# Weight loads moved behind the last row sums, and a lower pace for the mixing between the heads, in a fused attention and mixing kernel

## The chip, the cores and the metric

The kernel runs on one core of one Trainium2 chip. The metric is the device time of one execution in microseconds (us); lower is better. Engines are named as in the profile: PE is TensorE (matmuls; PEld are its weight loads), DVE is VectorE, ACT is ScalarE, POOL is GpSimd, and SP is the engine whose queue issues most of the DMAs.

## What is computed

Three steps follow each other. First comes causal attention with a decay bias, for 4 batches of 8 heads, 576 positions and 64 channels a head. Then a gated mixing with a convolution of five taps, and a second mixing with a product over positions, both on 4 x 576 x 512 numbers:

```python
cum = np.cumsum(np.maximum(s, 0.0), axis=-1)
scores = np.where(causal, -1e9, scale * (q @ k.T) + np.minimum(-(cum[..., :, None] - cum[..., None, :]), 0.0))
attn = softmax(scores)            # exp, divided by the row sums + 1e-9
x = attn @ v                      # heads side by side: [4, 576, 512]
gate = sigmoid(conv5(x, conv_w))
x = (gate * (x @ w_val)) @ w_out
h = relu(x @ w_in)                # [4, 576, 1024]
u, v = h[..., :512], h[..., 512:]
v_n = (v - mean(v)) / sqrt(var(v) + 1e-6)
v_s = einsum('ts,bsd->btd', w_spatial, v_n) + b_spatial
out = (u * v_s) @ w_out2
```

## The kernel before, in words

The 32 heads go through a pipeline, one head per step w (lines 673 to 713 of before). In step w the kernel makes the scores of head w (`scores`), transposes the weights p of head w-1 (`transposes`), and, in every second step, finishes the pair of heads before: it lays the row sums out (`lay_sums`: a transpose psr on PE, a copy rt on ACT, a small DMA that writes them to r_d in DRAM), reads them back spread over 64 partitions (`spread_sums`: two DMAs into R), multiplies weights and values (`pv`), scales the product by R into x, and adds up the convolution z (`conv`). Heads from number 8 on are prepared one step ahead (`prep`) in fp32r, as a high and a low part: their operands lie in qk, cn and kd, two buffers of each.

`pv` takes two heads at a time. Its twelve fp32 matmuls have 64 stationary columns each; those of the first head write partitions 0 to 63, those of the second 64 to 127. One matmul of it has two records in the profile. The numbers of output columns are 128 (into psq), 448, 448, 320, 192 and 64 (into pso) for each head.

Between these pieces the kernel does the mixing of the batch before. `mixing_a` casts x into high and low parts (xvh, xvl), multiplies them by four chunks of w_val and gates the products (gt, g). `mixing_b` makes v (four groups of 512 columns), normalises it, makes u, multiplies v over the positions (the spatial step), gates again (y) and multiplies by four chunks of the output weights (the output step, `ot`, with a DMA to the result). All of it is three fp32r matmuls for one product (high x high, low x high, high x low; `three`). Both functions are generators; they yield the cost in units after each group of 12 to 14 matmuls, some 60 units a batch. `more(n)` adds n units to what is due and takes groups off the queue until it is used up. In each step w five calls share n_g units; n_g is chosen by w (line 681). A batch's mixing is queued in the step after its last head (w = 9, 17, 25); that of the last batch follows the heads. What is not done when the heads end is done after them.

The calls only set an order of writing. The kernel is built with a scheduler (`schedule_with_timeline_sim=True`), which lays out each engine's instructions anew (the mixing is written under `tc.high_priority(offset=0)`). Each engine then works in its order.

Weight chunks come from DRAM, 128 x 1024 words each, into the two buffers wv (`load_chunk`). Those that are wanted after the heads are loaded ahead (lines 714 and 715): `load_ahead` takes a list of homes. "wv" are the two usual buffers; "pt" are the two buffers of the transposed weights of the heads, whose last reader is `pv`; "qk" are the two buffers of the heads' operands; cn and kds are two more pairs of operand tiles, which take a chunk in two halves of 128 x 512 words. `weight_chunk` picks up what was loaded ahead.

`LAST` remembers an instruction: before, only the last score reduction on DVE, behind which the first weight preparations are issued (`paced`, with `tc.issue_after`). `issue_after(ins)` puts every instruction of its block that runs on the engine of `ins` behind `ins` in that engine's order.

Of the kernel before, what the change touches and what calls it, by code (L numbers as in the profile page):

```python
# [24 lines left out]
def tile_stickbreak_attention_moe(  # L25
# [19 lines left out]
    B = out.shape[0]  # L45
    H = NH // B
# [11 lines left out]
    BLK, w = {}, 0  # L58
# [5 lines left out]
    V, G, A, T, SY = nc.vector, nc.gpsimd, nc.scalar, nc.tensor, nc.sync  # L64
# [45 lines left out]
    cn = [early.tile([128, S], F32R, name=f"cn{i}") for i in range(2)]  # L110
    kds = [early.tile([128, S], F32R, name=f"kd{i}") for i in range(2)]
# [16 lines left out]
    r_d = dram.tile([NH // 2, 2, 5, 128], F32, name="r_d")  # L128
    wv_d = dram.tile([NP, 128, 2, 512], F32, name="wv_d")
    wo_d = dram.tile([NP, 128, 2, 512], F32, name="wo_d")  # L130
# [8 lines left out]
    def load(h, cum=None):  # L139
        if h >= NH:  # L140
            return
        raw[h] = r = RAW[h % 2]
        src = qk2[h].rearrange("p (t s) -> p t s", t=2)
        if h < NATIVE:
            SY.dma_start(r[0:64], src[0:64])
            if h:
                if h < 3:
                    SY.dma_start(r[64:65, 0, :], f(cn[0][64:65]))
                SY.dma_start(r[64:65, 1, :], one_d[h:h + 1] if cum is None else cum[h:h + 1])
        else:  # L150
            SY.dma_start(r, src)
        vraw[h] = early.tile([128, 5, D], F32, tag="vraw", name="vraw", bufs=4)
        SY.dma_start(vraw[h], vp[h].rearrange("p (c d) -> p c d", c=5))
# [24 lines left out]
    LAST = {}  # L178
# [43 lines left out]
    R = {}  # L222
# [16 lines left out]
    def spread_sums(p):  # L239

        R[p] = early.tile([128, 5, 128], F32, tag="R", name="R", bufs=2)
        for j in range(2):
            SY.dma_start(R[p][64 * j:64 * j + 64].rearrange("p i q -> p (i q)"),
                         r_d[p, j].rearrange("i q -> (i q)").partition_broadcast(64))

    def evac_split(dst_hi, dst_lo, src):
        A.activation(dst_hi, src, AF.Copy)
# [160 lines left out]
    KC = list(range(NP))  # L408
# [43 lines left out]
    def load_chunk(src, mc, home="wv"):  # L452
        if home == "wv":
            w = mid.tile([128, 2, 4, 128], F32R, tag="wv", name="wv", bufs=2)
        elif home == "pt":
            w = early.tile([128, PTW], F32R, tag="pt", name="wpt", bufs=2)
        elif home == "qk":
            w = early.tile([128, 2, S], F32R, tag="qk", name="wqk", bufs=2).rearrange("p t s -> p (t s)")
        else:
            w = [t[:, 0:512].rearrange("p (k m) -> p k m", k=4) for t in home]  # L460
            for t in range(2):
                SY.dma_start(f(w[t]), src[mc, :, t].rearrange("p (k m) -> p k m", k=4))
            return w
        if home != "wv":
            w = w[:, 0:1024].rearrange("p (t k m) -> p t k m", t=2, k=4)
        SY.dma_start(f(w), src[mc].rearrange("p t (k m) -> p t k m", k=4))
        return w[:, 0], w[:, 1]
# [3 lines left out]
        key = src is wo_d, b, mc  # L471
        return AHEAD.pop(key) if key in AHEAD else load_chunk(src, mc)

    def load_ahead(src, b, homes):

        for mc, home in zip(KC, homes):
            AHEAD[src is wo_d, b, mc] = load_chunk(src, mc, home)

    def gated_split(dh, dl, psrc, other):
# [8 lines left out]
    def mixing_a(b):  # L488

        xh, xl = [], []  # L490
        for p in KC:
            xh.append(mid.tile([128, S], F32R, tag=f"xvh{p}", name=f"xvh{p}"))
            xl.append(mid.tile([128, S], F32R, tag=f"xvl{p}", name=f"xvl{p}"))
            hi_of(A, xh[p], X[b, p])
            lo_of(V, xl[p], X[b, p], xh[p])
        z = Z[b]
        if b < B - 1:
            A.activation(z, z, AF.Sigmoid)
        else:
            for p in KC:  # L500
                A.activation(z[:, p, :], z[:, p, :], AF.Sigmoid)
        g = GT[b] = mid.tile([128, NP, 2 * S + 64], F32R, tag="g", name="g")
        gh, gl = g[:, :, 0:S], g[:, :, S + 64:]
        for mc in KC:
            wh, wl = weight_chunk(wv_d, mc, b)
            for hf in range(2):
                pt = ps.tile([128, 512], F32, tag="m", name="psm", bufs=2)
                three(pt[:, 0:HS], KC, lambda kc: (wh[:, kc, :], wl[:, kc, :]),
                      lambda kc: (xh[kc][:, hs[hf]], xl[kc][:, hs[hf]]))
                gated_split(gh[:, mc, hs[hf]], gl[:, mc, hs[hf]], pt[:, 0:HS], z[:, mc, hs[hf]])  # L510
                yield 1.44

    def mixing_b(b):
        if b == B - 1:
            load_ahead(wo_d, b, ["wv", "wv", "pt", "pt"])
# [83 lines left out]
    def more(n):  # L599
        with tc.high_priority(offset=0):  # L600
            more_(n)
# [45 lines left out]
    def start():  # L647

        m = mixing_a(0)
        yield from both(m, first, 2)  # L650
        m = mixing_b(0)
        yield from both((next(m) for _ in range(5)), second_steps())
        for ec in range(4):
            fold(ec, 0)
            yield 2.56
        open_late()
        yield from both((next(m) for _ in range(8)), third_steps())
        yield from m
# [14 lines left out]
    for w in range(NH + 1):  # L673
        if w == H + 1:
            queue.clear()
            queue.append(start())
        elif w % H == 1 and w > 1 and w < NH:
            queue += [mixing_a(w // H - 1), mixing_b(w // H - 1)]
        if w >= NATIVE:
            load(w + 2)  # L680
        n_g = [3, 11.5, 10.0, 9.0, 9.5][0 if w <= H else 1 if w <= H + 4 else 2 if w <= 2 * H else 3 if w <= 3 * H else 4]
        gs = [n_g / 5] * 5
        if w < NH:
            scores(w, [0, 1])
        if w > 0:
            transposes(w - 1, [1, 2])
        if w % 2 == 0 and w > 0:
            lay_sums(w // 2 - 1)
        more(gs[0])
        if w < NH:  # L690
            scores(w, [2])
        prep(w + 1)
        if w > 0:
            transposes(w - 1, [3])
        more(gs[1])
        if w < NH:
            scores(w, [3])
        if w > 0:
            transposes(w - 1, [0])
        if w % 2 == 0 and w > 0:  # L700
            spread_sums(w // 2 - 1)
        more(gs[2])
        if w < NH:
            scores(w, [4])
            if w < NATIVE:
                load(w + 2)
            if w % 2:
                normalise(w // 2)
        more(gs[3])
        if w % 2 == 0 and w > 0:  # L710
            pv(w - 2)
            conv((w - 2) // H, ((w - 2) % H) // 2)
        more(gs[4])
    load_ahead(wo_d, B - 2, ["wv", "wv", "pt", "pt"])
    load_ahead(wv_d, B - 1, ["qk", "qk", cn, kds])
    queue += [mixing_a(B - 1), mixing_b(B - 1)]
    while queue:
        more(1)
# [50 lines left out]
```

## Time and profile before

| | |
|---|---|
| median of 3 runs | 536.41 us (533.68 to 536.85) |
| the profiled execution, its own time | 538.75 us |
| its span, first to last instruction | 537.0 us |
| PE busy | 503.1 us (94%), 3206 matmul records |
| ACT, DVE, POOL busy | 342.9 (64%), 314.0 (58%), 126.1 us (23%) |
| mean granted TensorE clock | 0.981 |
| moved by DMA | 71.36 MB, 133 GB/s over the span |

How to read it: a matmul's record is longer than the distance to the next one, because matmuls are pipelined. What a matmul costs PE is therefore read as the distance between the starts of two neighbours. Idle time before an instruction stands in square brackets, with the instruction that ended it. The clock is the share of 2.4 GHz that was granted.

### The profile page before, as it was taken

The numbers are of one execution on the slowest core, as the hardware profiler recorded it, in microseconds if no ns is written. First come the engines' busy times: TensorE is split into PE (matmuls) and PEld (weight loads), VectorE is DVE, ScalarE is ACT, GpSimd is POOL, SyncE is SP. The second block draws the span as 40 slices with busy tenths as digits, with TensorE's granted clock in tenths as the row PEclk, the third lists the DMA queues.
The fourth block names the chain that finished last, engine by engine and source line by source line (L and its number), as shares of the span: only waits on it lengthen the run. The fifth ranks groups of instructions, "written<-read, shape, count | busy, mean of one in ns | idle before, by whom it ended". The sixth has DMA issues, their size and how long they took to land.

```text
span 537.0 us, 9116 instructions
## 1 busy us (share of the span) xinstructions
PE 503.1 (94%) x3206; PEld 417.2 (78%) x3206; DVE 314.0 (58%) x836; ACT 342.9 (64%) x821; POOL 126.1 (23%) x166
## 2 busy tenths in 40 slices
PE   8777988999989999999999999999999999299997
PEld 4344655788768898988889898888789987298997
DVE  5778589788988865624886464565545541325120
ACT  3897679798678764954666475684867655234322
POOL 5220130016450112203351120032501300135240
PEclk9999889999999999999999999999999999689999
DMA  6949655437662633285331305763030178500002
GB/s 186 282 130 260 189 180 156 153 100 260 198 228 77 193 94 106 80 256 179 115 94 56 105 10 166 233 200 118 13 95 12 37 212 271 179 0 2 1 0 89
DMA packets 28910, 71.36 MB, mean 133 GB/s; under 512 B 4096, under 2 KB 12448, under 8 KB 28864
## 3 DMA queue, kind: packets, MB, share of 16 engines
q1 hardware_dynamic: 23936, 65.98, 40.6%
q10 hardware_dynamic: 4928, 4.80, 2.7%
q8 instruction: 25, 0.41, 0.3%
q14 instruction: 21, 0.17, 0.1%
HBM read 58.06 MB, written 9.16 MB: 125 GB/s over the span
## 4 chain that ended last, share of the span: by engine, by line
PE 64%; ACT 13%; DMA 12%; DVE 7%; issue 3%; SPq 1%; ACTq 0%; POOL 0%; DVEq 0%
PE psm L404 11%; PE psm L406 10%; PE psm L405 10%; PE pso L285 7%; PE pst L266 6%; PE psm L576 3%; PE psm L577 3%; PE psm L578 3%; ACT p L219 3%; DMA wg<-in_w_in 3%; PE pss L206 3%; DMA wr<-in_w_out 2%; PE pss L207 2%; ACT pt L267 2%; DMA R<-r_d 2%
## 5 line engine op out<-in xcount | busy, mean ns | idle before, releaser
L219 ACT ACTIVATE p<-p,nm 64x64 f32<-64x64 f32 (+4 forms) x160 | 88.6, 555 | 10.5 <-DVE nm L214 10.2
L266 PE MATMUL pst<-ident,p 128*128 128x128 f32 x480 | 77.6, 276 | 7.4 <-ACT pt L267 4.6
L214 DVE CUSTOM_DVE_ANT_0 p<-pss,mask 64x64 f32<-64x64 f32 (+4 forms) x160 | 64.3, 419 | 30.3 <-PE pss L207 19.2
L267 ACT ACTIVATE pt<-pst 128x512 f32<-128x512 f32 (+1 forms) x128 | 61.9, 494 | 21.8 <-PE pst L266 13.1
L266 PEld LDWEIGHTS pst<-ident,p 128*128 128x128 f32 x480 | 57.0, 141 | 22.8 <-ACT pt L267 8.2
L285 PE MATMUL pso<-pt,vraw 128*64 128x448 f32 (+3 forms) x320 | 66.1, 438 | 2.0 <-ACT pt L267 2.0
L301 DVE SCALAR_TENSOR_TENSOR z<-x,cw,z 128x575 f32<-128x575 f32 (+1 forms) x64 | 55.5, 867 | 6.9 <-ACT z L298 6.4
L79 POOL TENSOR_TENSOR g<-gt,g 128x288 fp32r<-128x288 f32 x32 | 28.5, 898 | 126.5 <-ACT g L72 126.5
L79 POOL TENSOR_TENSOR y<-gt,y 128x288 fp32r<-128x288 f32 x32 | 27.1, 845 | 108.9 <-ACT y L72 108.8
L206 PE MATMUL pss<-qk 128*64 128x64 f32 (+1 forms) x144 | 45.6, 333 | 1.1 <-DVE nm L214 1.1
L285 PEld LDWEIGHTS pso<-pt,vraw 128*64 128x64 f32 x320 | 28.4, 140 | 18.3 <-issue 8.7
L207 PE MATMUL pss<-kd,cn 66*64 66x64 f32 (+1 forms) x144 | 41.9, 296 | 0.0
L404 PE MATMUL psm<-g,wch 128*128 128x288 f32 x128 | 39.1, 306 | 0.0
L576 PE MATMUL psm<-wsh,vh 128*128 128x288 f32 x128 | 38.5, 303 | 0.0
L405 PE MATMUL psm<-g,wcl 128*128 128x288 f32 x128 | 37.8, 296 | 0.0
L406 PE MATMUL psm<-g,wch 128*128 128x288 f32 x128 | 37.7, 296 | 0.0
L577 PE MATMUL psm<-wsh,vl 128*128 128x288 f32 x128 | 37.5, 295 | 0.0
L578 PE MATMUL psm<-wsl,vh 128*128 128x288 f32 x128 | 37.5, 295 | 0.0
L404 PE MATMUL psm<-y,wv 128*128 128x288 f32 x112 | 34.3, 306 | 0.6 <-ACT pt L267 0.4
L481 DVE TENSOR_TENSOR gt<-psm,u 128x288 f32<-128x288 f32 x32 | 14.5, 454 | 34.7 <-PE psm L580 24.2
L406 PE MATMUL psm<-y,wv 128*128 128x288 f32 x112 | 33.1, 297 | 0.0
L405 PE MATMUL psm<-y,wv 128*128 128x288 f32 x112 | 32.9, 295 | 0.0
(171 smaller groups left out, 1310.9 us busy)
## 6 DMA issues: line engine op xcount, KB each, us to landing
raw<-in_qk SPq DMA_DIRECT2D x24, 576.0 KB
wv<-wo_d SPq DMA_DIRECT2D x16, 512.0 KB
wv<-wv_d SPq DMA_DIRECT2D x12, 512.0 KB
vraw<-in_vp SPq DMA_DIRECT2D x32, 160.0 KB
R<-r_d SPq DMA_DIRECT2D x32, 160.0 KB
out<-ot ACTq DMA_DIRECT2D x32, 144.0 KB
cn<-qk SPq DMA_DIRECT2D x24, 144.0 KB
wr<-in_w_in SPq DMA_DIRECT2D x5, 512.0 KB
```

Of the source, the lines that this page charges most:

```text
L79: eng.tensor_tensor(out=out_, in0=in_, in1=f(hi), op=ALU.subtract)
L206: T.matmul(pst[0:m, o:o + b - a], qa[:, q0:q0 + m], kb[:, a:b], start=True, stop=False)
L214: LAST["V"] = V.tensor_tensor_reduce(out=p[i][0:m, a:b], in0=src, in1=mask[0:m, o:o + b - a], scale=-0.125, scalar=3.0e38 if a == 0 else n ...
L219: A.activation(p[i][0:m, 0:e], p[i][0:m, 0:e], AF.Exp, bias=nm[0:m, i:i + 1], scale=-1.0, accum_out=sm[h // 2 % 2][0:m, h % 2, i:i + 1])
L266: T.transpose(pt[:, o - o0:o - o0 + 128], p[i][:, c * 128:(c + 1) * 128], ident[:, r:r + 128])
L267: A.activation(PT[h][:, o0:end], pt[:, 0:end - o0], AF.Copy)
L285: T.matmul(po[64 * j:64 * j + 64, a - q0:q1 - q0], vs[j][:, c, :], pts[j][:, o:o + q1 - a], start=c == 0, stop=c == cs[-1])
L301: V.scalar_tensor_tensor(out=z[:, d:], in0=x[:, :S - d], scalar=cw[:, p, k:k + 1], in1=z[:, d:], op0=ALU.mult, op1=ALU.add)
L404: T.matmul(pt, ah, bh, start=j == 0, stop=False)
L405: T.matmul(pt, al, bh, start=False, stop=False)
L406: T.matmul(pt, ah, bl, start=False, stop=j == n - 1)
L576: T.matmul(o, vh[c][:, cs], wsh[:, c, hs[hf]], start=c == 0, stop=False)
```

## The change

Two numbers of the pace become lower: steps 17 to 24 have 7.6 units each in place of 9.0, steps 25 to 32 have 6.0 in place of 9.5. `spread_sums` keeps its last DMA in `LAST["R"]`. `load_ahead` takes a list of chunks as well, so that the third batch's output chunks 0 and 1 (into wv) can be loaded as before, and chunks 2 and 3 (into pt), with the last batch's four chunks of w_val, stand in a block that SP issues behind the last R.

```diff
-            SY.dma_start(R[p][64 * j:64 * j + 64].rearrange("p i q -> p (i q)"),
-                         r_d[p, j].rearrange("i q -> (i q)").partition_broadcast(64))
+            LAST["R"] = SY.dma_start(R[p][64 * j:64 * j + 64].rearrange("p i q -> p (i q)"),
+                                     r_d[p, j].rearrange("i q -> (i q)").partition_broadcast(64))
...
-    def load_ahead(src, b, homes):
+    def load_ahead(src, b, homes, mcs=KC):
-        for mc, home in zip(KC, homes):
+        for mc, home in zip(mcs, homes):
             AHEAD[src is wo_d, b, mc] = load_chunk(src, mc, home)
...
-        n_g = [3, 11.5, 10.0, 9.0, 9.5][...]
+        n_g = [3, 11.5, 10.0, 7.6, 6.0][...]
...
-    load_ahead(wo_d, B - 2, ["wv", "wv", "pt", "pt"])
-    load_ahead(wv_d, B - 1, ["qk", "qk", cn, kds])
+    load_ahead(wo_d, B - 2, ["wv", "wv"])
+    with tc.issue_after(LAST["R"].ins):
+        load_ahead(wo_d, B - 2, ["pt", "pt"], KC[2:])
+        load_ahead(wv_d, B - 1, ["qk", "qk", cn, kds])
```

On SP's queue, at the end of the heads, this stood before (R is the read of the row sums, wo_d the output weights, wv_d those of w_val; wqk and wpt are chunks in the qk and pt buffers):

```order
L243 DMA R<-r_d 64x640 x2
L466 DMA wqk<-wv_d 128x1024
L462 DMA cn_96<-wv_d 128x512
L462 DMA kd_98<-wv_d 128x512
L466 DMA wv<-wo_d 128x1024 x3
L466 DMA wqk<-wv_d 128x1024
L466 DMA wv<-wo_d 128x1024
L462 DMA cn_97<-wv_d 128x512
L462 DMA kd_99<-wv_d 128x512
L466 DMA wv<-wo_d 128x1024 x2
L466 DMA wpt<-wo_d 128x1024 x2
L243 DMA R<-r_d 64x640 x2
```

And this stands there now:

```order
L243 DMA R<-r_d 64x640 x4
L466 DMA wqk<-wv_d 128x1024 x2
L462 DMA cn_96<-wv_d 128x512
L462 DMA cn_97<-wv_d 128x512
L462 DMA kd_98<-wv_d 128x512
L462 DMA kd_99<-wv_d 128x512
L466 DMA wpt<-wo_d 128x1024 x2
L466 DMA wv<-wo_d 128x1024 x2
L466 DMA wpt<-wo_d 128x1024 x2
```

The reads of the last two pairs' row sums now follow each other, and all early chunks stand behind them.

On PE, in the pv of heads 28 and 29 (the last pair but one; L404 to L406 are products of the mixing, psm their result), this stood before at its end:

```order
L405 MATMUL psm_4898<-y_4560,wv_4896 128x288
L406 MATMUL psm_4898<-y_4560,wv_4896 128x288
L285 MATMUL pso_4963<-pt_4813,vraw_4252 64x320
L285 MATMUL pso_4963<-pt_4635,vraw_4060 64x192
L285 MATMUL pso_4963<-pt_4813,vraw_4252 64x192
L285 MATMUL pso_4963<-pt_4635,vraw_4060 64x64
L285 MATMUL pso_4963<-pt_4813,vraw_4252 64x64
L207 MATMUL pss_4997<-kd1_99,cn1_97 128x192
```

In the same pv stands now:

```order
L285 MATMUL pso_4367<-pt_4095,vraw_3580 64x320
L404 MATMUL psm_4338<-wch_63,g_3993 128x512
L285 MATMUL pso_4367<-pt_4234,vraw_3764 64x320
L405 MATMUL psm_4338<-wch_63,g_3993 128x512
L285 MATMUL pso_4367<-pt_4095,vraw_3580 64x192
L406 MATMUL psm_4338<-wcl_64,g_3993 128x512
L285 MATMUL pso_4367<-pt_4234,vraw_3764 64x192
L404 MATMUL psm_4338<-wch_63,g_3993 128x512
L285 MATMUL pso_4367<-pt_4095,vraw_3580 64x64
L405 MATMUL psm_4338<-wch_63,g_3993 128x512
L285 MATMUL pso_4367<-pt_4234,vraw_3764 64x64
```

Matmuls of pv and products of the mixing now alternate one by one, and the mixing beside this pv is an earlier step of it (v in place of the output step).

On PE, behind the last pv of all, this stood before (the first products of the last batch's mixing follow at once):

```order
L285 MATMUL pso_5125<-pt_5087,vraw_4623 64x192
L285 MATMUL pso_5125<-pt_5006,vraw_4434 64x64
L285 MATMUL pso_5125<-pt_5087,vraw_4623 64x64
L404 MATMUL psm_5196<-xvh3_5170,wqk_5150 128x288
L405 MATMUL psm_5196<-xvh3_5170,wqk_5150 128x288
```

And now:

```order
L285 MATMUL pso_4875<-pt_4784,vraw_4385 64x192
L285 MATMUL pso_4875<-pt_4681,vraw_4222 64x64
L285 MATMUL pso_4875<-pt_4784,vraw_4385 64x64
L578 MATMUL psm_4892<-wsl_1733,vh2_4480 128x288
L576 MATMUL psm_4892<-wsh_1732,vh3_4533 128x288
L577 MATMUL psm_4892<-wsh_1732,vl3_4534 128x288
```

Products of the third batch's spatial step follow the last pv in place of the last batch's first products.

## Rows read from the trace of the kernel before

**Rows 1.** The page: busy times, and PE and its clock in 40 slices.
```profile
PE 503.1 (94%) x3206; PEld 417.2 (78%) x3206; DVE 314.0 (58%) x836; ACT 342.9 (64%) x821; POOL 126.1 (23%) x166
...
PE   8777988999989999999999999999999999299997
...
PEclk9999889999999999999999999999999999689999
```

**Rows 2.** Table by stretch: us, busy per engine (instructions), clock, DMA share, GB/s.
```profile
255.00:455.00 200.00, 198.85 (x1361) 172.11 (x1361) 110.63 (x295) 131.03 (x312) 42.62 (x54) 1.00 0.38 116
455.00:465.00 10.00, 0.26 (x4) 0.13 (x2) 1.49 (x4) 1.35 (x2) 0.00 (x0) 0.73 0.78 246
465.00:473.10 8.10, 7.01 (x28) 6.66 (x29) 4.34 (x8) 3.19 (x5) 2.68 (x3) 0.50 0.00 2
473.10:537.00 63.90, 60.77 (x412) 57.74 (x411) 15.05 (x30) 19.64 (x42) 19.52 (x27) 1.00 0.06 19
```

**Rows 3.** The same table (PE, PEld, DVE, ACT, POOL), two stretches among the heads.
```profile
350.00:360.00 10.00, 9.89 (x72) 8.90 (x73) 6.41 (x22) 8.97 (x25) 4.68 (x6) 1.00 0.63 194
380.00:390.00 10.00, 9.40 (x60) 7.55 (x59) 7.11 (x20) 7.34 (x19) 5.92 (x9) 1.00 0.08 17
```

**Rows 4.** PE's waits (us, times, longest): 255 to 455 us, then behind it.
```profile
PE pst L266 <- ACT p L219: 0.6, 1, 0.6
...
PE psm L404 <- ACT xvh L72: 9.7, 1, 9.7
PE psm L404 <- DVE gt L481: 1.1, 1, 1.1
```

**Rows 5.** Chain of waits at the heads' end: start, length, what.
```profile
451.52 4.82 DMA r_d<-rt
...
456.86 5.69 DMA R<-r_d
...
462.67 0.90 DVE x L289 x3
...
463.59 0.78 ACT z L298
...
467.89 0.61 PE psm L404
```

**Rows 6.** PE's timeline around a short pv run: start, length of the records.
```profile
431.79 0.29 PE L405 MATMUL psm<-y,wv 128*128 128x288 f32 x1
432.01 0.97 PE L285 MATMUL pso<-pt,vraw 128*64 128x448 f32 x4
432.91 0.41 PE L406 MATMUL psm<-y,wv 128*128 128x288 f32 x1
433.15 0.29 PE L404 MATMUL psm<-y,wv 128*128 128x288 f32 x1
433.28 0.29 PE L405 MATMUL psm<-y,wv 128*128 128x288 f32 x1
```

**Rows 7.** PE's timeline: the last pv and what follows it.
```profile
452.34 0.97 PE L285 MATMUL pso<-pt,vraw 128*64 128x448 f32 x4
453.14 0.39 PE L285 MATMUL psq<-pt,vraw 128*64 128x128 f32 x4
...
464.99 0.61 PE L404 MATMUL psm<-xvh,wqk 128*128 128x288 f32 x1 [9.74 <-ACT xvh L72]
...
468.53 0.45 PE L406 MATMUL psm<-xvl,wqk 128*128 128x288 f32 x1
468.77 0.45 PE L404 MATMUL psm<-xvh,wqk 128*128 128x288 f32 x1
```

**Rows 8.** Chain of waits early in the run: one pair's row sums.
```profile
94.79 1.93 DMA r_d<-rt
...
97.26 3.85 DMA R<-r_d
```

**Rows 9.** SP's timeline: the issue right ahead of the last R.
```profile
455.22 0.80 SPq L466 DMA_DIRECT2D wpt<-wo_d  x2
```

More of the change, by code (lines that the diff above doesn't have):

```diff
@@ L680, in tile_stickbreak_attention_moe @@
             load(w + 2)
-        n_g = [3, 11.5, 10.0, 9.0, 9.5][0 if w <= H else 1 if w <= H + 4 else 2 if w <= 2 * H else 3 if w <= 3 * H else 4]
+        n_g = [3, 11.5, 10.0, 7.6, 6.0][0 if w <= H else 1 if w <= H + 4 else 2 if w <= 2 * H else 3 if w <= 3 * H else 4]
         gs = [n_g / 5] * 5
```

## The prediction

> **What bounds the kernel now.** I read the busy times and the 40 slices first. TensorE (PE) works 94% of the span, and there is one hole: slice 35 shows 2 tenths, and the granted clock falls in it and in the next [rows 1]. Then the table by stretch: from 255 to 455 us PE is busy 198.85 of 200 us at clock 1.00, while ACT has 131 and DVE 111, so this part (most of the last sixteen heads, with the mixing between them) is a TensorE stretch. From 455 to 465 us PE has 0.26 us of work, from 465 to 473.1 us it runs 28 matmuls at clock 0.50 (the lower level, 1.2 GHz), and from there on it is at 1.00 again [rows 2]. The list of PE's waits says what the hole is: 9.7 us for the cast xvh of the last batch and 1.1 us for gt; in the 200 us before, the largest is 0.6 us [rows 4]. The chain of waits gives the way there: the write of the row sums r_d takes 4.82 us, their read back into R 5.69 us, then come x, the convolution's first step z and the cast; the first matmul after the second wait starts at 467.89 us [rows 5]. So the loss at the end of the heads is: 9.74 us idle (the number in the brackets of the row at 464.99), 1.09 us idle, and 28 matmuls that start 0.24 us apart (468.53 to 468.77) where at full clock they start 0.13 apart (433.15 to 433.28): 28 x 0.107 = 3.0 us [rows 2, 4, 6, 7]. Together 13.8 us, 2.6% of the time.
>
> **Part 1, the pacing: what it wins.** The budgets of heads 17 to 24 and from 25 on fall from 9.0 and 9.5 units to 7.6 and 6.0. Every matmul is still run, but less of the third batch's mixing lies between the heads. In the built order the last product of weights and values (pv) is followed by 172 matmuls of that mixing (76 of the spatial step, 96 of the output step) before the first of the last batch. At 0.133 us each that is 22.9 us of PE work. From the write of the row sums to the first matmul after the second wait the chain took 467.89 - 451.52 = 16.4 us [rows 5], and the last pv itself lies in that time too. So the hole is covered, and the clock's fall goes with it, since PE does not rest: gain 13.8 us. I find nothing that is late next: the last batch's casts xvh take the buffers of the spatial step's operands, free 96 matmuls (12.8 us) before they are wanted; eight operations (casts on ACT, subtractions on DVE) of about the 0.78 us of the ACT step in the chain [rows 5] fit in that on one engine even.
>
> **Part 1: what the new order costs.** The scheduler has laid out everything behind about 255 us anew, and this is the term that I weigh most. A pv consists of twelve fp32 matmuls of 64 columns of the array each, six for one head and six for the other, on the two halves of the array. Neighbours on different halves run side by side: of the run of eleven that begins at 452.34 us the first two, each of 448 output columns and two records, are over in 0.80 us together [rows 7]. Alone, or in a short run, they are dear: between products of the mixing stands a run of one 448 and one 320 (the second hidden beside the first). From the product at 431.79 to the second product behind it, at 433.15, are 1.36 us; less the two products' 0.27 the run costs 1.09 us [rows 6]. Some 0.76 us of this is streaming (the 0.80 with its start taken off; 1.7 ns a column), so that entering and leaving cost 0.33 us. A run of pv matmuls thus costs 0.33 us plus 1.7 ns for each column of its longer half. From the first place where PE's order differs, the order has 83 pv matmuls in 26 unbroken runs before and the same 83 in 52 runs now: in four of seven pv calls a mixing matmul now stands between nearly every two of the later ones. Entering and leaving: 26 x 0.33 = 8.6 us. Columns that stream with no partner grow from 7.3 to 14.3 thousand; 7.0 thousand x 1.7 ns / 2 (two that could have shared) = 5.9 us. Sum 14.5 us, all of it on PE where PE sets the pace, so on the path. Single mixing matmuls between transposes or scores I cost at nothing: pv alone splits the array.
> The Trainium skill (TensorEngine Tiling (Array Packing), Key Properties) says that changing the tiling mode drains the engine, and that different tiles work in parallel; it gives no price. The trace agrees with both, with the 0.33 and the 0.80 us above. If only the second held and a switch were free, the sum below would be -6.9 us.
> Bounds: 5.9 us (lost partners alone, if something hid the switches), and 17.9 us if each of the 26 added runs were a 448 made alone (1.09 - 0.40). I take 14.5, which both groups of rows show directly.
>
> **Part 1: waits among the heads.** With less mixing between them, the heads' own dependences could show. The trace has no stretch with this mixture, so I bound it. Below: PE is idle 1.15 us of the 200, so no more can be won. Above: the worst ten microseconds that I found there, 380 to 390 us, leave PE 0.60 us idle [rows 3]; the stretch will be about 200 - 22.9 + 14.5 = 192 us long, and if all of it were like that, it would be 11.5 us, 10.4 more than now. The nearest row is 350 to 360 us, where ACT is busy 8.97 of 10 and PE still 9.89 [rows 3]; ACT's share of the whole stretch stays at two thirds. I take +1.0 us.
>
> **Part 2, the loads behind the row sums.** Two chunks of the output weights for the pt buffers and the last batch's four chunks for its first product are now issued behind the last R. On SP's queue these are eight transfers of 3 MB by their shapes (128x1024 and 128x512 words). Before, two pt chunks stood right ahead of the last R [rows 9] and more chunks were in flight; r_d and R took 4.82 + 5.69 = 10.5 us [rows 5] against 1.93 + 3.85 = 5.8 us early in the run [rows 8], while the DMA moved 246 GB/s [rows 2]. So the late issue shortens the chain by up to 4.7 us. I enter it with 0: PE has 22.9 us of other work meanwhile, and the pacing alone would cover the longer chain too. Without that cover it would be worth its 4.7 us.
> The Trainium skill (DMA: Bandwidth & Descriptors, Issuing engines are not separate DMA queues) says that transfers of all issuing engines interleave on the same 16 engines; that the 5 KB write from ACT's queue took 4.82 us beside SP's loads agrees. By this rule alone one would book 4.7 us more.
> The other side: what waits behind R? The pt chunks are wanted 124 matmuls after the last pv, 16.5 us later. Up to the end of the first of them 2.5 MB must land: at 246 GB/s 10.2 us. It fits, so 0. At the 116 GB/s that moved on average from 255 to 455 us [rows 2] it would be 21.6 us, and PE would wait 5.1 us.
>
> **Sum.** -13.8 + 14.5 + 1.0 = +1.7 us. On the profiled execution (span 537.0, its own time 538.75) that is 540.4. This execution is 2.3 us above the median of the runs shown, 536.41; the same difference on the median gives 538.1.
>
> **Rivals.** (a) Faster: the hole closes and the switches cost nothing, because they fall where PE would have waited for a weight load or an operand anyhow; PE's small waits go as well. -13.8 + 5.9 - 1.2 = -9.1, 527.3 us. For it: a scheduler breaks a run where it sees a reason. Against: PE has 1.15 us idle in that stretch, there is next to nothing to hide in. Chance 0.13.
> (b) Slower: the heads starve PE. Mixing is what PE does while DVE and ACT turn scores into weights; at 6.0 units a head the two score buffers, the two transpose buffers and the preparation of the next head's operands (which waits for the last read of kd and cn) set the pace. At the bound above: -13.8 + 14.5 + 10.4 = +11.1, 547.5 us; from 4.7 us of new waits on the kernel is slower by over 1%. For it: the pv term has eaten the gain already, so little is needed. Against: PE at 9.89 beside the busiest ACT. Chance 0.20.
> (c) Slower, the loads come too late: the wait of 5.1 us and a fall of the clock like the old one, 3.0 us: +9.8, 546.2 us. Against: 246 GB/s were reached in just such a stretch. Chance 0.04.
> That the change does not do what it says would be a hole that stays; 172 matmuls in the built order speak against it, and it gets no share.
>
> **Numbers.** The forecast has 0.63. A measurement of this kernel can tell about 1%, 5.4 us, from no change: faster is below 531.0, slower above 541.8. (a) lies in the first, (b) and (c) in the last: 0.13, 0.63 and 0.24. The range runs from 529 to 546: it takes in half of the way to (a) and most of the way to (b) and (c), and leaves out their far ends.
>
> **What would show it.** Right: no hole at the end of the heads and the clock at 1.00 in all late slices; lone pv matmuls of 448 columns that cost PE about 1.09 us; PE busy over 99% through the heads; the last matmul within 3 us of where it was. Wrong: lone pv matmuls that cost no more than their streaming (then a); PE idle for tenths of a microsecond again and again at scores and transposes (then b); a wait for wpt or wqk after the last pv (then c).

## The result and the profile after

The changed kernel takes 540.67 us (median of 10 executions, 537.66 to 541.43) against 536.85 us (10 executions, 533.68 to 539.75) of the kernel before: ratio 1.0070, 95% interval 1.0045 to 1.0095. The forecast was 538.1 us, 0.3% above before, most likely within 1%; it is 0.7% above, 3.8 us.

The page after (busy times, then the 40 slices of PE and its clock), which answers to [rows 1]:

```profile
PE 517.1 (97%) x3206; PEld 419.1 (78%) x3206; DVE 316.4 (59%) x836; ACT 340.1 (63%) x819; POOL 128.4 (24%) x166
...
PE   7989998999999999999999999999998999999997
...
PEclk9689999999999999999999999999998999999999
```

The hole in slice 35 is gone and the clock stays up at the end; what is left is one small dent in slice 31 in both rows. PE is busy 517 us in place of 503, with as many matmuls: it has no more to do, it takes longer over it. The table by stretch shows the same (compare [rows 2]: 0.26 us of PE work from 455 to 465 us, clock 0.50 behind it):

```profile
255.00:455.00 200.00, 197.31 (x1235) 158.60 (x1234) 111.86 (x291) 125.05 (x300) 43.36 (x53) 0.99 0.32 99
455.00:465.00 10.00, 9.50 (x71) 9.27 (x71) 0.77 (x1) 2.32 (x6) 0.15 (x1) 1.00 0.69 190
465.00:473.10 8.10, 8.10 (x63) 8.10 (x62) 1.83 (x4) 1.86 (x6) 2.43 (x3) 1.00 0.54 172
473.10:537.00 63.90, 59.42 (x403) 56.38 (x402) 14.59 (x29) 19.57 (x42) 19.59 (x27) 1.00 0.06 19
```

In the first stretch PE is busy 197.31 us over 1235 records, before it was 198.85 us over 1361. A PE that looks as busy as before gets through 126 matmul records fewer there (the two windows stand at different places of the work, so this is a pace and no count of the same matmuls). PE's waits from 249.9 us on (total, times, longest) answer to [rows 4]; the waits of 9.7 and 1.1 us are gone:

```profile
PE pss L206 <- DVE nm L214: 1.8, 1, 1.8
PE pst L266 <- ACT p L219: 0.9, 1, 0.9
PE psm L404 <- ACT ot L591: 0.5, 1, 0.5
```

**The balance.** PE's order is the same in both kernels up to a place that stands at 255.1 us in the profiled execution of before and at 249.9 us in that of after. This common part differs by 5.2 us between two executions of the same instructions, so the two profiled executions (538.75 and 537.66 us) can't be set against each other as they are; from that place on they can. For it I added up what PE's order costs when nothing waits: each product, transpose and score by the distance between neighbouring starts at clock 1.00 (0.133 us for a product of 288 columns, 0.233 for 512, 0.108 for a transpose), each unbroken run of pv by 0.335 us plus 1.67 ns for each column of its longer half. I call this sum PE's work.

| from the first difference to the last matmul, us | before | after | difference | forecast |
|---|---|---|---|---|
| time | 278.5 | 282.4 | +3.9 | +1.7 |
| PE's work by its order | 260.8 | 275.4 | +14.6 | +14.5 |
| rest in the stretch with the hole | 14.4 | 0 | -14.4 | -13.8 |
| rest elsewhere (waits, low clock) | 3.3 | 6.9 | +3.7 | +1.0 |

The rows are rounded one by one. The +3.9 us of this balance, from one execution each, agree with the +3.8 us of the medians.

**Where the 14.6 us are.** PE's timeline in the pv of heads 28 and 29, where products and pv matmuls alternate:

```profile
384.15 0.96 PE L285 MATMUL pso<-pt,vraw 128*64 128x448 f32 x2
385.05 0.49 PE L406 MATMUL psm<-wcl,g 128*128 128x512 f32 x1
385.47 0.75 PE L285 MATMUL pso<-pt,vraw 128*64 128x320 f32 x2
...
389.47 0.33 PE L285 MATMUL pso<-pt,vraw 128*64 128x64 f32 x2
389.73 0.50 PE L405 MATMUL psm<-wch,g 128*128 128x512 f32 x1
390.15 0.33 PE L285 MATMUL pso<-pt,vraw 128*64 128x64 f32 x2
```

From the lone 448 to the next pv matmul are 1.32 us; less the product's 0.233 it cost 1.09 us, the price that [rows 6] gave for a short run. A lone 64 costs 390.15 - 389.47 - 0.23 = 0.45 us; 0.11 of that is its columns, 0.34 the entering and leaving. The page counts all of this as busy.

**Where the 3.7 us are.** Of after's rest of 6.9 us, 3.7 lie between 407 and 415 us; the other 3.2 are as much as before had outside of the hole. PE's timeline there:

```profile
407.46 0.60 PE L266 MATMUL pst<-ident,p 128*128 128x128 f32 x4
409.89 0.40 PE L206 MATMUL pss<-qk 128*128 128x288 f32 x1 [1.84 <-DVE nm L214]
...
411.10 0.44 PE L406 MATMUL psm<-g,wch 128*128 128x288 f32 x1
411.34 0.44 PE L404 MATMUL psm<-g,wch 128*128 128x288 f32 x1
...
414.17 0.29 PE L404 MATMUL psm<-g,wch 128*128 128x288 f32 x1
414.30 0.29 PE L405 MATMUL psm<-g,wcl 128*128 128x288 f32 x1
```

A score waits 1.84 us for its buffer, which the score reduction on DVE frees. The scores that are reduced there (320 columns) had left PE by 406.5. Behind the wait the products start 0.24 us apart (411.10 to 411.34) until about 414 us, then 0.13 again: an estimated 1.6 us more, by the number of matmuls in that stretch. The table by stretch gives the clock of it, and DVE's timeline what the reduction stood behind:

```profile
405.00:410.00 5.00, 3.16 (x24) 2.89 (x23) 4.75 (x16) 3.49 (x11) 2.01 (x3) 1.00 0.15 33
410.00:415.00 5.00, 5.00 (x27) 4.89 (x28) 2.66 (x9) 4.64 (x13) 0.78 (x2) 0.66 0.01 2
```

```profile
406.45 0.76 DVE L79 TENSOR_TENSOR qk<-raw,qk 64x576 fp32r<-64x576 f32 x1
407.24 0.75 DVE L79 TENSOR_TENSOR kd<-raw,qk 64x576 fp32r<-64x576 f32 x1
407.91 0.68 DVE L537 BATCH_NORM_STATS2 bs<-v 64x6 f32<-64x512 f32 x1
408.51 0.93 DVE L227 TENSOR_SCALAR den<-sm 128x10 f32<-128x10 f32 x1
409.36 0.47 DVE L214 CUSTOM_DVE_ANT_0 p<-pss,mask 128x320 f32<-128x320 f32 x1
```

DVE is busy 4.75 of the 5 us: the preparation of the next head's operands (qk and kd, 1.5 us together), the mixing's statistics (L537) and the row sums' den (L227) run ahead of the reduction for which PE waits.

The clock's fall does not always follow this wait. pace_alone, the first of the experiments below, has the same wait of 1.83 us, and the products behind it start 0.13 us apart from the first on:

```profile
412.97 0.40 PE L206 MATMUL pss<-qk 128*128 128x288 f32 x1 [1.83 <-DVE nm L214]
414.14 0.29 PE L404 MATMUL psm<-g,wch 128*128 128x288 f32 x1
414.28 0.30 PE L405 MATMUL psm<-g,wcl 128*128 128x288 f32 x1
```

So of the 3.7 us the wait is the part that both traces have; how many of the ten timed executions of the change had the low clock as well is not known.

### The profile page after: what moved, and what is told of

The parts are those of the page before. It is cut to its first block, busy times and chain, and to the rows that moved or that the text cites. A ratio compares the mean times of both kernels' runs of the same rounds, so it can differ in the third digit from the quotient of the medians.

```text
span 535.9 us, 9097 instructions
## 1 busy us (share of the span) xinstructions
PE 517.1 (97%) x3206; PEld 419.1 (78%) x3206; DVE 316.4 (59%) x836; ACT 340.1 (63%) x819; POOL 128.4 (24%) x166
## 2 busy tenths in 40 slices
DMA packets 28334, 69.27 MB, mean 129 GB/s; under 512 B 4032, under 2 KB 12384, under 8 KB 28288
## 4 chain that ended last, share of the span: by engine, by line
PE 66%; ACT 12%; DMA 11%; DVE 5%; issue 3%; SPq 2%; POOL 1%; ACTq 0%; DVEq 0%; POOLq 0%
PE psm L404 11%; PE psm L406 10%; PE psm L405 10%; PE pso L285 9%; PE pst L266 6%; PE psm L576 3%; PE psm L578 3%; PE psm L577 3%; ACT p L219 3%; DMA wr<-in_w_out 3%; PE pss L206 2%; DMA wg<-in_w_in 2%; PE pss L207 2%; ACT pt L267 2%; DMA r_d<-rt 2%
## 5 line engine op out<-in xcount | busy, mean ns | idle before, releaser
L285 PE MATMUL pso<-pt,vraw 128*64 128x448 f32 (+3 forms) x320 | 74.8, 431 | 1.1 <-ACT pt L267 1.1
L266 PEld LDWEIGHTS pst<-ident,p 128*128 128x128 f32 x480 | 58.1, 141 | 17.8 <-ACT pt L267 5.9
L79 POOL TENSOR_TENSOR y<-gt,y 128x288 fp32r<-128x288 f32 x32 | 28.2, 882 | 119.0 <-ACT y L72 119.0
L404 PE MATMUL psm<-g,wch 128*128 128x288 f32 x128 | 40.0, 314 | 0.0
L406 PE MATMUL psm<-g,wch 128*128 128x288 f32 x128 | 38.5, 303 | 0.0
L481 DVE TENSOR_TENSOR gt<-psm,u 128x288 f32<-128x288 f32 x32 | 14.4, 455 | 37.6 <-PE psm L580 28.2
L481 DVE TENSOR_TENSOR gt<-psm,z 128x288 f32<-128x288 f32 x32 | 14.3, 452 | 35.4 <-PE psm L406 31.7
L206 PEld LDWEIGHTS pss<-qk 128*64 128x64 f32 (+1 forms) x144 | 26.0, 182 | 9.8 <-DVE nm L214 4.2
L72 ACT ACTIVATE y<-gt 128x288 fp32r<-128x288 f32 x32 | 14.1, 439 | 28.3 <-DVE gt L481 28.3
```

What stands on the lines that cost most here:

```text
L79: eng.tensor_tensor(out=out_, in0=in_, in1=f(hi), op=ALU.subtract)
L206: T.matmul(pst[0:m, o:o + b - a], qa[:, q0:q0 + m], kb[:, a:b], start=True, stop=False)
L266: T.transpose(pt[:, o - o0:o - o0 + 128], p[i][:, c * 128:(c + 1) * 128], ident[:, r:r + 128])
L285: T.matmul(po[64 * j:64 * j + 64, a - q0:q1 - q0], vs[j][:, c, :], pts[j][:, o:o + q1 - a], start=c == 0, stop=c == cs[-1])
L404: T.matmul(pt, ah, bh, start=j == 0, stop=False)
L406: T.matmul(pt, ah, bl, start=False, stop=j == n - 1)
```

## The experiments

Twelve kernels ran. Theory A is the balance above: the time moves with PE's work (which the splitting of pv raises) and with the hole. Against it stand that the late loads cost or win (B), that the pace itself starves PE through the heads and the runs were broken where PE would have waited anyhow (C), and that with a faster PE the other engines, the loads and the clock's falls set the time (D). Ratios are against before, run beside each on the same chip, with 95% intervals. "Behind" counts PE's instructions behind the last pv; 456 of them are the last batch's own mixing (in before 18 of these stand ahead of the last pv), and what is above 456 covers the way of the last row sums.

| kernel | paces | pv runs | PE's work, whole order, us | behind | median us | ratio |
|---|---|---|---|---|---|---|
| before | 9.0, 9.5 | 61 | 463.8 | 438 | 536.85 | 1 |
| the change | 7.6, 6.0 | 87 | 478.4 | 628 | 540.67 | 1.0070 (1.0045 to 1.0095) |
| pace_alone | 7.6, 6.0 | 86 | 477.3 | 632 | 539.17 | 1.0087 (1.0058 to 1.0117) |
| loads_alone | 9.0, 9.5 | 61 | 463.8 | 456 | 533.00 | 0.9979 (0.9959 to 0.9998) |
| tight_on_change | 7.6, 6.0 | 34 | 447.2 | 636 | 523.90 | 0.9824 (0.9775 to 0.9873) |
| tight_on_before | 9.0, 9.5 | 31 | 445.5 | 456 | 538.29 | 1.0077 (1.0051 to 1.0103) |
| tight_late | 7.6, 6.0 | 40 | 450.8 | 636 | 524.17 | 0.9768 (0.9687 to 0.9848) |
| tight_late_front | 7.6, 6.0 | 41 | 451.9 | 626 | 518.75 | 0.9707 (0.9655 to 0.9759) |
| pv_priority | 7.6, 6.0 | 62 | 463.5 | 623 | 530.71 | 0.9910 (0.9868 to 0.9953) |
| tight_late_mid_pace | 8.2, 6.4 | 39 | 451.0 | 566 | 512.48 | 0.9609 (0.9534 to 0.9684) |
| mid_pace_early_loads | 8.2, 6.4 | 39 | 451.0 | 566 | 514.27 | 0.9622 (0.9597 to 0.9648) |
| mid_pace_no_edge | 8.2, 6.4 | 83 | 476.0 | 567 | 535.53 | 1.0027 (1.0008 to 1.0047) |
| front_high_pace | 8.6, 7.2 | 43 | 453.4 | 492 | 534.76 | 0.9983 (0.9952 to 1.0015) |
| front_old_pace | 9.0, 9.5 | 38 | 450.1 | 456 | 534.22 | 0.9963 (0.9923 to 1.0003) |

### One part of the change at a time

pace_alone is before with the two new paces and nothing else:

```diff
-        n_g = [3, 11.5, 10.0, 9.0, 9.5][...]
+        n_g = [3, 11.5, 10.0, 7.6, 6.0][...]
```

> The two lower paces alone; the loads stand where they stood before. Theory A (PE is the bound, and the broken pv runs are the price): in the built order the pv matmuls of the whole kernel stand in 86 runs (before 61, the change 87), which by 0.335 us a run and 1.7 ns per column of a run's longer half is 13.5 us more PE work than before; the hole at the end of the heads is covered (-14 us); some 3 us of waits among the heads: 537 to 542 us, within 0.5% of the changed kernel. Theory B (the price is in the loads behind the last R): without them the kernel gains the hole, 523 to 530 us.

Measured: 1.0087, 539.17 us, as theory A has it; it overlaps with the change's 1.0070. The pace alone makes the result; the late loads add nothing that shows.

loads_alone is the change with the old paces, 9.0 and 9.5, so only the loads are moved.

> The late loads alone; the pace stays at 9.0 and 9.5. PE's order is that of before up to the last head, pv in 61 runs as before. Theory A: the hole stays, but r_d and R no longer queue behind weights, so that the chain through them is up to 4.7 us shorter: 531 to 536 us. Theory B: the weights that now come after R make PE wait: slower than before, 538 us and more, with a wait for wqk or wpt.

Measured: 0.9979, 533.00 us, in theory A's range but hardly to be told from no change. PE's longest wait (total, times, longest) is still the hole, but its last cause has changed:

```profile
PE psm L404 <- DMA wqk<-wv_d: 8.6, 1, 8.6
```

The late loads did shorten the way of the row sums here: from the issue of r_d to the first product with R it takes 7.8 us, 11.2 before. But now the chunk wqk that was moved behind R arrives last. The hole goes from 9.74 to 8.6 us: a shorter chain was won, and the moved load took its place.

One thing in this is particular to the old pace. There the third batch's output step is over within the heads (at 448.08 us in before), so the four output chunks that are loaded ahead for it are read by nobody: before has 20 loads of wo_d (16 into wv, 4 into wpt) for 16 chunks that matmuls read, the change has 16.

```profile
wv<-wo_d SPq DMA_DIRECT2D x16, 512.0 KB
wv<-wo_d SPq DMA_DIRECT2D x12, 512.0 KB
```

The first line is before's, the second the change's; the DMA moved 71.36 and 69.27 MB. Two of the unread chunks are the wpt that stand right ahead of the last R in [rows 9]; in loads_alone they stand behind R and ahead of the wqk for which PE waits 8.6 us (issued at 448.73 and 449.37, wqk at 449.79). The lower pace thus also takes 2.1 MB out of the DMA at the heads' end. What the late loads would win at the old pace without these four chunks was not tried.

### pv kept together

If the broken runs cost the 14.6 us, an order that keeps them whole must win them back. Two edges (a note to the scheduler that one instruction stands behind another) do this on PE: pv is issued behind the last product that was written ahead of it (front), and the mixing behind it waits in the order for pv's last matmul (rear). tight_on_change puts both on the change, tight_on_before the same on before (the last product of the spatial step is kept in `LAST["M"]` in the same way, not shown):

```diff
-            T.matmul(po[...], vs[j][:, c, :], pts[j][...], start=..., stop=...)
+            with tc.issue_after(LAST["M"]) if "M" in LAST else ExitStack():
+                LAST["pv"] = T.matmul(po[...], vs[j][:, c, :], pts[j][...], start=..., stop=...).ins
...
-            T.matmul(pt, ah, bl, start=False, stop=j == n - 1)
+            LAST["M"] = T.matmul(pt, ah, bl, start=False, stop=j == n - 1).ins
...
-            more_(n)
+            with tc.issue_after(LAST["pv"]) if "pv" in LAST else ExitStack():
+                more_(n)
```

> The changed kernel, and order edges on PE alone (no waits): a pv's matmuls are issued behind the last mixing product written before them, and the mixing written later is issued behind that pv. pv stands in 34 runs in place of 87. Theory A: PE work falls by 31 us (0.335 us a run, 1.7 ns per column of the longer half): 508 to 516 us, if up to 6 us of new waits come. Theory C (the thin filling is what costs, and the runs were broken where PE would have waited anyhow): the edges only turn work into waits, 537 us and more, with PE idle among the heads rising by some 20 us.

> The kernel before with the same order edges; pv in 31 runs in place of 61. Theory A: PE work falls by 18 us, the hole of 14 us at the end of the heads stays: 517 to 524 us, and the change on top of it (the third kernel here) is faster by 4 to 12 us, since it then pays no broken runs for the hole. Theory C: 536 us and more.

Measured: on the change 523.90 us, 2.4% less than the change by the two ratios, with the same matmuls and paces; that lies between theory A (508 to 516) and theory C (537 and more). On before 538.29 us, 0.8% slower, though PE's work fell by 18.3 us. Theory A alone falls here: it asked for 517 to 524 us, and theory C's 536 and more is what came. PE's waits of tight_on_before from 200 us on say where the gain went:

```profile
PE psm L405 <- ACT xvh L72: 8.5, 1, 8.5
PE psm L405 <- DMA wv<-wv_d: 2.9, 2, 2.7
PE psm L405 <- ACT u L565: 2.3, 1, 2.3
PE psm L405 <- DVE gt L482: 2.2, 2, 1.1
```

The hole stays at the old pace (nothing but the last batch's own mixing is behind the last pv), and a PE that is through its work sooner now waits for weight chunks, for u on ACT and for gt on DVE, with a fall of the clock behind the longer waits (0.95 on average from 340 to 375 us). So theory C's outcome came at the old pace and not at the new one: PE's work sets the time only as long as the other engines and the loads keep up.

Three milder ways to keep pv together, all on the change: both edges only for heads from 16 on (tight_late), only the front edge for these heads (tight_late_front: the condition of the first line becomes `"M" in LAST and h >= 16`, the rear edge is left out), and no edge but a higher rank in the scheduler (pv_priority):

```diff
-            pv(w - 2)
+            with tc.high_priority():
+                pv(w - 2)
```

> The changed kernel with the order edges around pv, for the heads from 16 on alone (the earlier ones stand as in the changed kernel). PE work by the built order is 27.6 us under the changed kernel's (pv in 40 runs, not 87). Theory A (PE work is the bound, waits stay as in the changed kernel): 0.949 of the changed kernel, so 0.956 of before, 511 us where before is 534.6. Theory D (with PE faster, ACT, DVE and the weight loads set the pace, and PE's waits and half-clock stretches take half back): 0.97 to 0.98 of before, 519 to 524 us. The edges on the early heads, which this kernel lacks, cost some 3 us in the kernel with all of them: faster than that one.

> As before, but only the front edge: a pv's matmuls are issued behind the last mixing product written before them; the mixing written later is free. PE work 26.5 us under the changed kernel's (41 runs). Theory A: 512 us. Theory D with the rigid order as the cause of waits: as the kernel with both edges or up to 3 us faster.

> The changed kernel with pv written at a high priority, no edges. In the built order pv stands in 62 runs (before 61, changed 87), PE work is 14.9 us under the changed kernel's, as much as before's, and 623 PE instructions still follow the last pv, so that the hole is covered. Theory A: the change then costs nothing and wins the hole: 0.972 to 0.98 of before, 520 to 524 us. If the broken runs were not the price (theory C), it would stand at 1.00 to 1.007 of before like the changed kernel.

Measured: 524.17, 518.75 and 530.71 us. All three miss theory A (511, 512 and 520 to 524 us); tight_late (0.9768) is as theory D has it (0.97 to 0.98). pv_priority is the cleanest test of the forecast's two large terms: it has before's PE work (463.5 against 463.8 us) and the covered hole, and is faster than before by 0.9%. That is 4.4 us of the 14 that the hole cost; its trace has four waits of transposes for the weights p (4.6 us together) and one for a weight chunk (1.4 us) in return; the rest was not followed up. Between the two edges and the front one alone the intervals touch, so what the rear edge costs stays open.

### How low the pace must be

With pv kept together by the front edge the pace can be tried by itself. tight_late_mid_pace has 8.2 and 6.4 units:

> The front edge for heads from 16 on, with paces 8.2 and 6.4 in place of 7.6 and 6.0. PE work as with 7.6 and 6.0 (39 runs), 566 PE instructions behind the last pv, which still cover the hole. Theory D: the heads get a little more filling, waits among them fall by 1 to 3 us; theory A: the same time as with the lower pace.

Measured: 512.48 us, ratio 0.9609: faster than both kernels of this case, 4% below before. Its page:

```profile
PE 490.0 (96%) x3206; PEld 414.0 (81%) x3206; DVE 313.6 (61%) x836; ACT 341.7 (67%) x821; POOL 126.3 (25%) x166
...
PE   7979988999999999998999999999999999999997
```

PE is busy 27 us less than in the change over the same matmuls, and has no hole.

Then the other end, the front edge with the old paces (front_old_pace), and a step between (front_high_pace, 8.6 and 7.2):

> The front edge for pv of heads from 16 on and the late loads, with the old paces 9.0 and 9.5. PE work is as small as with 8.2 and 6.4 (pv in 38 runs), but only the last batch's mixing is left behind the last pv, so the hole stays. If the pace is worth the hole once pv stays together (theory A with D): some 10 to 13 us slower than with 8.2 and 6.4, 0.98 to 0.985 of before. If the pace was worth nothing and all of the win came from the runs: the same as with 8.2 and 6.4, 0.961.

> The same with paces 8.6 and 7.2: PE work 2.4 us more than with 8.2 and 6.4 (43 runs), and 36 matmuls of the third batch's mixing, 4.8 us, behind the last pv, against 110 (14.6 us) with 8.2 and 6.4. The hole of about 9 us that the late loads alone left is then half covered: 3 to 8 us slower than with 8.2 and 6.4, 0.967 to 0.976 of before, with a wait of PE of some 4 us for wqk or xvh.

Measured: 0.9963 and 0.9983. So once pv is whole the lower pace is worth 3.5% (0.9963 to 0.9609, some 19 us), more than the 10 to 13 us that I had expected of it. Seen from the other side, at the old pace the front edge wins nothing that shows (0.9963 against 0.9979 of loads_alone), though PE's work is 13.7 us less. And the step between, expected at 0.967 to 0.976, missed: it is no better than the old pace. PE's waits of the two from 200 us on, first front_old_pace:

```profile
PE psm L405 <- DMA wqk<-wv_d: 9.1, 1, 9.1
PE psm L405 <- DMA wv<-wv_d: 3.5, 2, 3.2
PE psm L405 <- ACT u L565: 2.3, 1, 2.3
```

and front_high_pace:

```profile
PE psm L405 <- DMA wv<-wo_d: 6.7, 3, 5.1
PE psm L405 <- DMA wpt<-wo_d: 3.3, 1, 3.3
PE psm L405 <- DMA wv<-wv_d: 2.9, 2, 2.4
```

The largest wait of front_high_pace, 5.06 us, stands ahead of the last pv (which begins at 448.23):

```profile
445.08 0.58 PE L405 MATMUL psm<-y,wv 128*128 128x288 f32 x1 [5.06 <-DMA wv<-wo_d]
```

SP stood at the last R until 437.50 us, and only behind it, from 438.63 on, it issued this output chunk of the third batch, one that the change does not move. The wait of 3.3 us comes behind the last pv: of the 36 matmuls (4.8 us) that are left there the last 24 need wpt, which is issued among the last batch's chunks at 451.66, and PE stands until 456.74. This second wait is rival (c) of the prediction, late loads that make PE wait, at a place where the cover is too thin. The clock averages 0.81 from 430 to 466 us there. Three chunks that nobody reads are loaded here too (70.84 MB). Time does not fall evenly with the pace: between 7.2 and 6.4 units is a step. With 8.2 and 6.4 units the whole output step lies behind the heads, all its chunks are wanted late and none is loaded in vain; which of these makes the step was not tried apart.

### The two parts of the best version

The last two runs take one thing away from tight_late_mid_pace each: the edge (mid_pace_no_edge, which is the change with paces 8.2 and 6.4), and the late loads (mid_pace_early_loads, the chunks issued as in before).

> The change with paces of 8.2 and 6.4 units in place of 7.6 and 6.0, and nothing else: pv is not kept together. Theory A (PE's work in the built order sets the time): the order has 83 runs of pv and 476.0 us of PE work, against 87 and 478.4 in the change and 39 and 451.0 in the version with the same paces and the front edge, so 538 us here, 0.3% above before or less. Rival (it is the pace that made the 512 us, not the unbroken pv): 514 to 520 us.

> The best version so far (front edge, paces 8.2 and 6.4) with the weight chunks issued ahead of the last row sums again, as before; PE's order is the same, instruction by instruction, with 110 matmuls (14.6 us) of the third batch's mixing behind the last pv. Theory: the cover is now about as long as the chain of the row sums; before, that chain took 16.4 us from the write of r_d to the first matmul, and the late loads shorten the read of R by some 5 us, so without them PE waits 2 to 4 us and the clock falls behind it: 514 to 518 us against 512.5, ratio 0.962 to 0.971. Rival (the late loads are worth nothing here either, as in the change): 512.5 us, ratio 0.957 to 0.961.

Measured: without the edge 535.53 us, ratio 1.0027, as theory A has it. The 512 us are not the pace's doing alone: the splitting of pv costs 4.2% at 8.2 and 6.4 units (1.0027 against 0.9609) and 3.6% at 7.6 and 6.0 (1.0070 against 0.9707), 22 and 19 us, where the difference in PE's work is 25.0 and 26.5 us. With the loads issued early 514.27 us: the ratio (0.9622) lies at the edge of the theory (0.962 to 0.971), its interval takes in the rival's too, and the trace decides for the rival. PE has no wait for xvh, and the way of the row sums is no longer. Here it is in mid_pace_early_loads (issue of r_d on ACT's queue, first product with R on DVE),

```profile
418.80 0.28 ACTq L237 DMA_DIRECT2D r_d<-rt  x1
424.96 0.34 DVE L290 TENSOR_TENSOR x<-psq,R 128x64 f32<-128x64 f32 x2
```

and here with the late loads, in tight_late_mid_pace:

```profile
415.41 0.28 ACTq L237 DMA_DIRECT2D r_d<-rt  x1
421.57 0.34 DVE L290 TENSOR_TENSOR x<-psq,R 128x64 f32<-128x64 f32 x2
```

6.16 us in both. At the lower pace the early chunks have landed before the row sums are written (SP issues the last of them at 412.49 us), so there is nothing to get out of the way.

## Why the prediction was right, step by step

**The hole (-13.8 us): right.** It is gone, with 14.4 us in the balance; nothing else was late in its place, as forecast. No trace with 110 or more matmuls of the third batch behind the last pv shows a hole there.

**Broken runs of pv (+14.5 us): right.** The order gave it, the price of [rows 6] holds in lone matmuls of 448 and of 64 columns, and the balance has 14.6 us. Every version with fewer runs of pv at the same pace is faster than the change: by the ratios 1.6% (pv_priority), 2.4% (tight_on_change), 3.0% (tight_late) and 3.6% (tight_late_front). Rival (a), broken runs that cost nothing, falls with that. But they give back less than PE's work fell: 9 us of 14.9, 13 of 31.2, 16 of 27.6 and 19 of 26.5. And "all of it on the path" holds at the new pace only, as tight_on_before and front_old_pace show. The Trainium skill (TensorEngine Tiling (Array Packing), Key Properties) says that a change of the tiling mode drains the engine; the 0.34 us around a lone 64 agree, but no run separates the draining from other causes. That "pv alone splits the array" was misread: scores too have a block with 64 stationary columns. Behind the product at 295.58 us in the changed kernel one starts at 295.72 and the next matmuls 0.03 and 0.05 us later, so nothing like 0.33 us shows there, and the sum is not touched.

**New waits among the heads (+1.0 us): the term that was mis-sized; it measured +3.7.** This is the step "I take +1.0 us", taken from PE's idle time beside the busiest ACT. The wait that came was not ACT's but DVE's, 1.84 us at one score, and I had priced idle time without the clock: in the profiled execution the products behind it ran at half speed for some 3 us and nearly doubled it. pace_alone has the same wait without the clock's fall, so the 1.8 us of the wait are the sure part, above the forecast by themselves; at 8.2 and 6.4 units (mid_pace_no_edge) PE has no wait for DVE. So rival (b) came true in small, at a third of its bound of 10.4 us. It is the preparation of the next head's operands, which rival (b) names, and the statistics and den that stood ahead of the reduction; why the scheduler placed them there was not tried.

**Late loads (0): right in the sum by luck, not in its reason.** I had written that the late issue shortens the chain by up to 4.7 us and that the cover hides this. At the old pace it did shorten it (11.2 to 7.8 us, loads_alone). At the new pace it doesn't: in the change it is 431.72 to 436.89, 5.2 us, but pace_alone with its early loads has 5.0 us. The lower pace had already put the four chunks of w_val ahead of the row sums (in pace_alone SP issues the last of them at 428.47 us, r_d follows at 433.52) and dropped the four output chunks that nobody read, the two of [rows 9] among them. The rule of the Trainium skill that I had weighed (DMA: Bandwidth & Descriptors, Issuing engines are not separate DMA queues), that transfers of all issuers interleave on the same engines, agrees with loads_alone; in pace_alone there was little to interleave with (DMA share 0.18 from 433.5 to 438.5 us, 0.91 in before from 456.3 to 462.7). The 2.5 MB that must land up to the first wpt are 2.6 by the shapes, 10.7 us in place of 10.2, which changes nothing. That wpt comes in time (rival c) held in the change: no wait for wpt or wqk shows in its waits. SP issues R and the chunks behind it:

```profile
432.99 1.09 SPq L243 DMA_DIRECT2D R<-r_d  x2
434.17 1.01 SPq L466 DMA_DIRECT2D wqk<-wv_d  x2
...
442.13 0.80 SPq L466 DMA_DIRECT2D wpt<-wo_d  x2
```

With 172 matmuls behind the last pv there was room; with 36 in front_high_pace the rival was real, 3.3 us of wait.

**The signs.** The hole that is gone, the lone 448 at 1.09 us and the missing waits for wpt and wqk came as named. Three signs of being right came only nearly: the clock has a dent in slice 31, PE is busy 98.7% and not over 99% in the first stretch, and by the balance the end moves by 3.9 us and not within 3.

**Left open.** Why the scheduler splits pv in the orders that it made was not found; the edges only forbid it. The waits of transposes for p or pt on ACT that versions with whole pv show (1.8 us at the longest, in tight_on_change and tight_late_front) were not tried separately.

## What to carry to other kernels

A lower pace for filler work closes a hole at the end only if the filler that is moved costs the same in its new place: where a scheduler lays out the order, count in the built order what gets interleaved with what, above all matmuls on a part of the array, before booking the gain. Then keep the expensive group together and tune the pace again, since the two depend on each other (0.9963 at the old pace and 1.0070 at the new one alone, 0.9609 for the two with the pace retuned). Choose the cover behind the last dependence longer than the loads that are issued there, and look for loads behind a waiting DMA on the same queue and for chunks that nobody reads any more. Price a wait on PE of some 2 us at its length and, as an upper end, at nearly double, since the clock fell behind some waits of this length and not behind others.

## What the runs showed of the hardware

- Entering and leaving a run of pv's 64-column fp32 matmuls between products costs some 0.335 us, for a short matmul as for a long one: the lone 64 and the lone 448 above leave 0.34 each, less their columns. The 64-column scores (fp32r operands) show nothing of the kind.
- The granted clock fell to its lower level (1.2 GHz; products 0.24 us apart, 0.66 on average from 410 to 415 us) behind an idle time of only 1.84 us. Behind 1.83 us in pace_alone it stayed at 1.00. Of two waits of 2.30 us for u it fell behind the one in tight_on_before (0.69 on average from 390.9 to 395.9 us) and not behind the one in front_old_pace (1.00 from 386.3 to 391.3 us). An idle time of about 2 us alone does not tell.
- The same instructions in the common first part, up to the first difference in PE's order, took 255.1 and 249.9 us in two executions, which is more than the change moved.
